# Recurrent segment attention beside a gated MLP: one projection moved to another group, small steps made list items, and new instruction lists

## Chip, cores, metric

One core of a Trainium2 chip. The metric is device time in microseconds for the whole program, the median of the runs. All weights and activations are bf16, sums are f32.

## The reference

x is 2048 tokens of 640 features. Two branches work on it and a gate mixes them.

```python
# A: 64 segments of 32 tokens, 32 heads of 192; 8 memory rows go from segment to segment
mem = mem0
for s in range(64):
    h = concat([mem, x[32 * s:32 * s + 32]])       # 40 rows
    q, k, v = h @ Wq, h @ Wk, h @ Wv               # 640 -> 32 heads x 192
    p = softmax(where(mask, q @ k.T / sqrt(192), -1e9))
    o = (p @ v) @ Wo                               # back to 640
    mem = o[:8]; out_s = o[8:]
# B: gated MLP, 640 -> 1536 -> 640
b = (gelu(x @ w_gate) * (x @ w_up)) @ w_down
g = sigmoid((x * gate_w).sum(-1))
return g * a + (1 - g) * b
```

Only the memory rows tie a segment to the one before, so the 64 segments are a serial chain. The mask lets the memory rows see everything and a token see the memory and the tokens up to itself.

## The kernel before

**Scheduler.** The source writes every operation with `S_.add(engine, ..., reads, writes)`, in one order for all engines. Each engine runs its own operations in that order; waits are derived from the regions read and written. Two engines that use one PSUM bank are always ordered, readers too. SP issues nearly all DMAs, in order as well, so an issue that waits holds those behind it. Every operation thus has a place in five queues: TensorE, ScalarE (ACT), VectorE (DVE), GpSimd (POOL) and SP.

**Stages.** First branch B runs in four blocks of 512 tokens (`ffn_transposes`, `ffn_gu`, `ffn_down`); its result goes to DRAM (`b_scr`), with the transposed x (`x_scr`, `xl_scr`) and the gate. Then come 64 calls of `segment(s)`.

**A segment.** A projection step works with 32 rows: the 8 memory rows that the segment before has just made, and the first 24 tokens. The last 8 tokens of each segment (the "left" rows) need no recurrence on the query side; they are projected for four segments at once, 32 rows at a time, and stored in DRAM (`qkl`). The 32 heads are four octets of 8 heads. `octet(s, i)` runs them forward in even segments and backward in odd ones, so i is the order in the segment. One projection of an octet, Q, K or V, has five pieces (k = 0 to 4) of 128 x 1536 weights; a piece is a quad: four matmuls of 384 columns, one for each 32-column strip of TensorE (L1121 where the stationary rows are loaded, L226 where they are kept from the matmul before).

**Lists.** `PROGS` holds four lists of items, one for each place of a segment in its group of four (place 1 is s % 4 == 0, place 4 is s % 4 == 3). An item is:

- `("g", n, k)`: piece k of every projection (m, i) in `GROUPS[n]`, with m = 0, 1, 2 for Q, K, V. They share one stationary: the first loads it, the others keep it. After the last k, ACT copies Q and K rows (L1141) and V (L1144) out of PSUM. In place 1 each V quad is followed by one for the left rows of V (`Vl`), copied by DVE (L1088).
- `("tq", i)`, `("tk", i)`: DVE transposes the rows of Q or K (L1155).
- `("sc", i)`: mask and scores (L1163, L1171, L1176), then on DVE maximum (L1189) and subtraction.
- `("ex", i)`: exponential on ACT, sum, reciprocal and product (L1207) on DVE.
- `("pt", i)`: TensorE transposes the probabilities; ACT copies them to PT.
- `("pv", i)`: P times V (L1254, L1256), into one PSUM bank (octet 3: two, A and B). ACT copies it to uT (L1265); in octet 3 DVE copies the middle third (L1270, "uT mid"). POOL then copies the left rows' part of uT into `uTl` (L1273).
- `("wo", i, h)`: output products of half an octet (L1283). Those of octet 3 go to a bank of their own (L1306). In place 4 every `wo` also multiplies `uTl` of four segments (`Wol`).
- `("lf", q, u, k)`: piece k of a left unit, that is Q and K of one octet for the left rows of the next group (L936, L226): two quads. `("le", q, u, m)`: ACT copies (L941) and DVE transposes (L943) it, SP stores it.
- `("vb", k)`: left rows of V for the next segment, in place 4.

**End of a segment.** The products of octets 0 to 2 lie in two halves of a bank: ACT copies one (`Zp`, L1289), DVE adds the other in two steps (`Zs`, L1292, `half_sums`), right behind item `("wo", 2, 1)`. After the list DVE adds octet 3's (`Za`, L1468) and transposes the memory rows (`Tm0`, L1472), on which the next segment's first quad waits; then the mix with b (`bz`) and the gate. What stands at the head of the next list as `lf`, or at the end of place 4 as `Wol`, is work that TensorE has meanwhile.

**Weights.** All weights but 16 pieces fit in SBUF at once. 13 pieces of Q, K and V of octet 0 share their space with the same pieces of octet 3, and three of Wo with three others; they are swapped in every segment by SP (L645) when TensorE has used them (`swap_loads`). Of one Q piece, `HALF`, only HX bytes per partition are swapped (L642). `out_store` and `x_load` are issued after the group with K of i = 1, `bz_load` and `bzl_load` (four DMAs) after the last `g` item.

## Time and profile before

| | us |
|---|---|
| Median of 3 runs | 1715.14 (1714.35 to 1719.47) |
| The profiled execution, its own time | 1719.43 |
| Its span, first to last instruction | 1717.6 |

| Engine | busy us | share |
|---|---|---|
| TensorE matmuls | 1589.8 | 93% |
| TensorE weight loads | 824.3 | 48% |
| VectorE | 955.7 | 56% |
| ScalarE | 800.4 | 47% |
| GpSimd | 340.2 | 20% |

The program moves 484.99 MB by DMA, 282 GB/s over the span. TensorE's granted clock is 0.997 on average. To read a profile row: the line of the kernel, engine and operation, then written and read tiles with their shapes; in groups a count, busy time and the mean in ns, and the idle time ahead of them with what ended it; in a timeline the start, the duration, and in square brackets the idle time ahead. [...]

### The profile page before, as it was taken

The page shows a single profiled execution, that of the slowest core. Times are in us where ns is not written, and L with a number is a line of the kernel's source. Part 1 is how long each engine was busy: PE and PEld are TensorE (multiplying, and loading weights), DVE is VectorE, ACT ScalarE, POOL GpSimd, SP SyncE. Part 2 cuts the span into 40 slices and gives each one's busy share as a digit, 9 for nine tenths or more (in the row PEclk, how much of TensorE's full clock was granted, in tenths as well). Part 3 has the DMA queues.
Part 4 walks back from the last instruction along what each step waited for, and adds up shares of the span by engine and source line. Part 5 has one row for each costly group of instructions (what it writes and reads, how often), then busy time and mean ns, then how long its engine had stood idle before and what let it go on. Part 6 is the DMA issues. An engine that isn't in the chain of part 4 may idle for free. (4 is left out here: it accounts for less than half of the span.)

```text
span 1717.6 us, 80494 instructions
## 1 busy us (share of the span) xinstructions
PE 1589.8 (93%) x39181; PEld 824.3 (48%) x31501; DVE 955.7 (56%) x2930; ACT 800.4 (47%) x1899; POOL 340.2 (20%) x1101
## 2 busy tenths in 40 slices
...
GB/s 326 316 53 137 290 303 310 291 265 288 299 303 292 274 300 292 322 280 277 275 305 311 276 309 269 302 301 280 288 286 299 296 305 265 297 292 310 275 278 258
DMA packets 273822, 484.99 MB, mean 282 GB/s; under 512 B 107686, under 2 KB 142782, under 8 KB 273470
## 3 DMA queue, kind: packets, MB, share of 16 engines
...
q14 instruction: 76, 0.62, 0.1%
...
## 5 line engine op out<-in xcount | busy, mean ns | idle before, releaser
L1121 PE MATMUL ps<-arena 128*32 128x384 bf16 x9940 | 710.0, 328 | 23.5 <-DVE arena L1472 12.3
L226 PE MATMUL ps<-arena 128*32 128x384 bf16 x7680 | 593.1, 327 | 12.7 <-ACT arena L1039 3.9
L1121 PEld LDWEIGHTS ps<-arena 128*32 128x32 bf16 x9940 | 253.8, 96 | 392.2 <-issue 259.6
L1155 DVE STREAM_TRANSPOSE arena<-arena 128x384 bf16<-128x384 bf16 x512 | 275.1, 561 | 149.4 <-ACT arena L1141 148.0
L1141 ACT ACTIVATE arena<-ps 128x384 bf16<-128x384 f32 x512 | 237.1, 490 | 223.9 <-PE ps L1121 210.0
L1283 PE MATMUL ps<-arena 128*32 128x320 bf16 x6144 | 278.5, 301 | 15.3 <-issue 12.7
L1265 ACT ACTIVATE arena<-ps 128x480 bf16<-128x480 f32 (+1 forms) x256 | 137.3, 536 | 174.8 <-PE ps L1256 163.8
L1283 PEld LDWEIGHTS ps<-arena 128*32 128x32 bf16 x6144 | 168.9, 107 | 72.6 <-issue 23.6
L1273 POOL COPY arena<-arena 128x96 bf16<-128x96 bf16 x256 | 89.9, 351 | 555.5 <-ACT arena L1265 506.7
L1144 ACT ACTIVATE arena<-ps 128x384 bf16<-128x384 f32 x256 | 125.1, 489 | 103.9 <-PE ps L1121 101.2
L1006 POOL COPY arena<-arena 128x96 bf16<-128x96 bf16 x256 | 68.4, 267 | 503.4 <-PE ps L1176 394.6
L1189 DVE TENSOR_REDUCE arena<-ps 104x4 f32<-104x160 f32 x256 | 82.7, 323 | 141.4 <-PE ps L1176 125.4
L1203 DVE TENSOR_REDUCE arena<-ps 104x4 f32<-104x160 f32 x256 | 80.6, 315 | 104.8 <-ACT ps L1201 102.5
L1239 ACT ACTIVATE arena<-ps 128x448 bf16<-128x448 f32 x192 | 104.0, 542 | 67.1 <-PE ps L1226 66.0
L1254 PE MATMUL ps<-arena 128*64 128x160 bf16 x1536 | 118.5, 243 | 6.8 <-ACT arena L941 3.3
L1201 ACT ACTIVATE ps<-ps 104x160 f32<-104x160 f32 x256 | 74.8, 292 | 102.6 <-DVE ps L1191 102.6
L1254 PEld LDWEIGHTS ps<-arena 128*64 128x64 bf16 x1536 | 79.6, 109 | 86.0 <-issue 28.7
L936 PE MATMUL ps<-arena 128*32 128x384 bf16 x1280 | 108.8, 328 | 0.1
L1256 PE MATMUL ps<-arena 128*64 128x64 bf16 x1536 | 102.0, 193 | 0.6 <-issue 0.6
L943 DVE STREAM_TRANSPOSE arena<-arena 128x384 bf16<-128x384 bf16 x128 | 73.0, 571 | 43.1 <-ACT arena L941 42.8
L1171 PE MATMUL ps<-arena 128*40 128x40 bf16 x2048 | 69.0, 182 | 26.3 <-DVE arena L1155 23.6
L1306 PE MATMUL ps<-arena 128*32 128x160 bf16 x3072 | 71.6, 233 | 23.0 <-DVE arena L1270 16.6
...
## 6 DMA issues: line engine op xcount, KB each, us to landing
...
arena<-in_A_Wq_dram SPq DMA_DIRECT2D x63, 144.0 KB, 3.3
...
```

Source lines behind the costliest of these rows:

```text
L226: return e.add_instruction(mybir.InstMatmult(name=nm, start_tensor_calc=like["start"], stop_tensor_calc=stop, tile_size=(128, 32), tile_po ...
L936: fns.append(lambda e, outp=outp, rhs=rhs, j=j: e.matmul(outp, lhs, rhs, start=(k == 0), stop=(k == KT - 1), tile_position=(0, 32 * j)))
L1121: fns.append(lambda e, outp=outp, rhs=rhs, j=j: e.matmul(outp, lhs, rhs, start=(k == 0), stop=(k == KT - 1), tile_position=(0, 32 * j)))
L1141: S_.add("act", lambda e, m=m, bk=bk: e.activation(out=rows_sb[m], in_=ps[:, bk, 0:384], func=ACTF.Copy), reads=[r_ps[bk]], writes=[r_rows ...
L1144: S_.add("act", lambda e, i=i, bk=bk: e.activation(out=v_sb[i % NVB].rearrange("p (c n) -> p c n", c=3), in_=ps[:, bk, 0:384].rearrange("p ...
L1155: S_.add("dve", lambda e: e.transpose(out=dst[:, :, 0:L], in_=rows_sb[m].rearrange("p (c r) -> p c r", r=L)), reads=[r_rows[m]], writes=[r ...
L1239: S_.add("act", lambda e: e.activation(out=PT, in_=ps[:, bank, 0:PTW + 128], func=ACTF.Copy), reads=[r_ps[bank]], writes=[r_PT], name="pT ...
L1254: return [lambda e: e.matmul(full, v[:, e0:e0 + 64], PTm[:, i], start=True, stop=False, tile_position=(0, 64 * i), skip_group_check=True), ...
L1256: lambda e: e.matmul(part, vl[:, e0:e0 + 64], PTl[:, i], start=False, stop=True, tile_position=(0, 64 * i), skip_group_check=True)]
L1265: S_.add("act", lambda e: e.activation(out=apx(u[:, 0, 0, :], [[R, na], [3 * R, 4], [1, R]]), in_=ps[:, A, 0:na * W].rearrange("p (c t r) ...
L1273: S_.add("pool", lambda e: e.tensor_copy(out=uTl[:, q, :, 12 * oc:12 * oc + 12].rearrange("p i (t c) -> p i t c", c=3), in_=u[:, :, :, L:R ...
L1283: fns.append(lambda e, i=i, t=t, j=j, gv=gv: e.matmul(ps[32 * j:32 * j + 32, bank, 0:2 * DJ].rearrange("p (h n) -> p h n", h=2), lhs2[i], ...
```

## The change

1. **Groups.** K of i = 2 joins the group of V of i = 1 and Q of i = 2: six groups instead of seven, and one load of the stationary per k less.
2. **uTl.** uT keeps the 32 token rows alone. The left rows go straight from PSUM to `uTl` by DVE, in place of POOL's copy from uT. The copy reads the bank that ACT reads for uT, and so comes after it.
3. **Items.** `zp` and `zs` (the two half sums), `ou` (`out_store`), `xt` (`x_load`) and `bz` (`bz_load`) are items with places of their own. `outl_store` follows `("sc", 2)` in place 1.
4. **Left rows of b.** `bl_copy` lays them out in DRAM (`bl_scr`) so that `bzl_load` is one DMA, now in place 4 after group 1.
5. **Left units.** Place 1 has none; its unit, octet 3, goes to place 3, which has two.
6. **Memory.** Freed space makes HX 384 instead of 1152 bytes.
7. **Prologue.** In block 0 the transposed x is copied out of PSUM after each 128 tokens, in turn from two sets of banks. The gate's DVE transposes (`gate_turn`) come after the third left unit instead of the first.
8. **New lists** for all four places.

The core of the diff; of the old lists their last lines only:

```diff
-    GROUPS = [[(0, 0), (1, 0)], [(2, 0), (0, 1), (1, 1)], [(2, 1), (0, 2)], [(1, 2)], [(2, 2), (0, 3)], [(1, 3)], [(2, 3)]]
...
-         ("g", 5, 2), ("g", 5, 3), ("wo", 0, 0), ("g", 5, 4), ("tq", 3), ("pt", 1), ("g", 6, 0), ("tk", 3),
-         ("lf", 0, 1, 0), ("lf", 0, 1, 1), ("ex", 2), ("pv", 1), ("sc", 3), ("wo", 0, 1), ("pt", 2), ("g", 6, 1),
-         ("lf", 0, 1, 2), ("ex", 3), ("pv", 2), ("lf", 0, 1, 3), ("g", 6, 2), ("g", 6, 3), ("g", 6, 4), ("pt", 3),
-         ("lf", 0, 1, 4), ("le", 0, 1, 0), ("wo", 1, 0), ("wo", 1, 1), ("pv", 3), ("wo", 2, 0), ("le", 0, 1, 1),
-         ("wo", 2, 1), ("wo", 3, 0), ("wo", 3, 1)],
...
-         ("wo", 0, 0), ("ex", 2), ("g", 5, 4), ("pv", 1), ("tk", 3), ("sc", 3), ("g", 6, 0), ("lf", 1, 1, 3),
-         ("pt", 2), ("wo", 0, 1), ("g", 6, 1), ("g", 6, 2), ("ex", 3), ("lf", 1, 1, 4), ("pv", 2), ("g", 6, 3),
-         ("pt", 3), ("g", 6, 4), ("wo", 1, 0), ("le", 1, 1, 0), ("wo", 1, 1), ("pv", 3), ("le", 1, 1, 1),
-         ("wo", 2, 0), ("wo", 2, 1), ("wo", 3, 0), ("wo", 3, 1)],
...
-         ("lf", 2, 1, 4), ("g", 5, 2), ("g", 5, 3), ("tq", 3), ("g", 5, 4), ("tk", 3), ("g", 6, 0), ("pt", 2),
-         ("g", 6, 1), ("sc", 3), ("le", 2, 1, 0), ("ex", 3), ("wo", 1, 0), ("g", 6, 2), ("pv", 2), ("wo", 1, 1),
-         ("wo", 2, 0), ("pt", 3), ("g", 6, 3), ("g", 6, 4), ("wo", 2, 1), ("pv", 3), ("le", 2, 1, 1), ("wo", 3, 0),
-         ("wo", 3, 1)],
...
-         ("tq", 3), ("g", 5, 1), ("g", 5, 2), ("g", 5, 3), ("g", 5, 4), ("wo", 0, 0), ("pt", 2), ("tk", 3),
-         ("g", 6, 0), ("sc", 3), ("g", 6, 1), ("wo", 0, 1), ("g", 6, 2), ("pv", 2), ("wo", 1, 0), ("ex", 3),
-         ("g", 6, 3), ("wo", 1, 1), ("g", 6, 4), ("vb", 0), ("vb", 1), ("pt", 3), ("wo", 2, 0), ("pv", 3),
-         ("wo", 2, 1), ("wo", 3, 0), ("wo", 3, 1), ("vb", 2), ("vb", 3), ("vb", 4)]]
+    GROUPS = [[(0, 0), (1, 0)], [(2, 0), (0, 1), (1, 1)], [(2, 1), (0, 2), (1, 2)], [(2, 2), (0, 3)], [(1, 3)], [(2, 3)]]
+        [("g", 0, 0), ("g", 0, 1), ("g", 0, 2), ("g", 0, 3), ("ou", 0), ("g", 0, 4), ("g", 1, 0), ("g", 1, 1),
+         ("tq", 0), ("g", 1, 2), ("tk", 0), ("sc", 0), ("g", 1, 3), ("ex", 0), ("g", 1, 4), ("g", 2, 0), ("g", 2, 1),
+         ("g", 2, 2), ("tq", 1), ("pt", 0), ("g", 2, 3), ("tk", 1), ("g", 2, 4), ("sc", 1), ("pv", 0), ("g", 3, 0),
+         ("g", 3, 1), ("g", 3, 2), ("g", 3, 3), ("tq", 2), ("tk", 2), ("ex", 1), ("sc", 2), ("g", 3, 4),
+         ("wo", 0, 0), ("pt", 1), ("g", 4, 0), ("ex", 2), ("g", 4, 1), ("g", 4, 2), ("g", 4, 3), ("g", 4, 4),
+         ("tq", 3), ("g", 5, 0), ("g", 5, 1), ("xt", 0), ("tk", 3), ("pv", 1), ("wo", 0, 1), ("pt", 2), ("sc", 3),
+         ("ex", 3), ("pv", 2), ("g", 5, 2), ("g", 5, 3), ("g", 5, 4), ("pt", 3), ("wo", 1, 0), ("wo", 1, 1),
+         ("bz", 0), ("pv", 3), ("wo", 2, 0), ("wo", 2, 1), ("zp", 0), ("wo", 3, 0), ("zs", 0), ("wo", 3, 1)],
+        [("lf", 1, 0, 0), ("lf", 1, 0, 1), ("lf", 1, 0, 2), ("g", 0, 0), ("g", 0, 1), ("g", 0, 2), ("g", 0, 3),
+         ("g", 0, 4), ("tq", 0), ("lf", 1, 0, 3), ("g", 1, 0), ("tk", 0), ("lf", 1, 0, 4), ("g", 1, 1),
+         ("le", 1, 0, 0), ("sc", 0), ("g", 1, 2), ("g", 1, 3), ("le", 1, 0, 1), ("ex", 0), ("ou", 0), ("g", 1, 4),
+         ("g", 2, 0), ("g", 2, 1), ("tq", 1), ("tk", 1), ("g", 2, 2), ("pt", 0), ("g", 2, 3), ("sc", 1), ("pv", 0),
+         ("ex", 1), ("g", 2, 4), ("wo", 0, 0), ("wo", 0, 1), ("xt", 0), ("g", 3, 0), ("g", 3, 1), ("pt", 1),
+         ("bz", 0), ("g", 3, 2), ("g", 3, 3), ("tk", 2), ("tq", 2), ("g", 3, 4), ("g", 4, 0), ("g", 4, 1), ("sc", 2),
+         ("g", 4, 2), ("tq", 3), ("g", 4, 3), ("g", 4, 4), ("tk", 3), ("g", 5, 0), ("lf", 1, 1, 0), ("ex", 2),
+         ("lf", 1, 1, 1), ("lf", 1, 1, 2), ("g", 5, 1), ("sc", 3), ("pv", 1), ("g", 5, 2), ("pt", 2),
+         ("lf", 1, 1, 3), ("ex", 3), ("lf", 1, 1, 4), ("le", 1, 1, 0), ("pv", 2), ("pt", 3), ("g", 5, 3),
+         ("g", 5, 4), ("le", 1, 1, 1), ("wo", 1, 0), ("wo", 1, 1), ("pv", 3), ("wo", 2, 0), ("wo", 2, 1), ("zp", 0),
+         ("wo", 3, 0), ("zs", 0), ("wo", 3, 1)],
+        [("lf", 2, 0, 0), ("xt", 0), ("lf", 2, 0, 1), ("g", 0, 0), ("lf", 2, 0, 2), ("g", 0, 1), ("lf", 2, 0, 3),
+         ("lf", 2, 0, 4), ("le", 2, 0, 0), ("g", 0, 2), ("g", 0, 3), ("g", 0, 4), ("tk", 0), ("tq", 0),
+         ("le", 2, 0, 1), ("g", 1, 0), ("g", 1, 1), ("g", 1, 2), ("g", 1, 3), ("g", 1, 4), ("sc", 0), ("g", 2, 0),
+         ("g", 2, 1), ("tq", 1), ("tk", 1), ("g", 2, 2), ("ex", 0), ("ou", 0), ("g", 2, 3), ("g", 2, 4), ("sc", 1),
+         ("tk", 2), ("g", 3, 0), ("pt", 0), ("g", 3, 1), ("g", 3, 2), ("tq", 2), ("ex", 1), ("g", 3, 3), ("pv", 0),
+         ("g", 3, 4), ("sc", 2), ("g", 4, 0), ("g", 4, 1), ("lf", 2, 1, 0), ("pt", 1), ("tq", 3), ("ex", 2),
+         ("g", 4, 2), ("lf", 2, 1, 1), ("g", 4, 3), ("wo", 0, 0), ("g", 4, 4), ("lf", 2, 1, 2), ("tk", 3),
+         ("lf", 2, 1, 3), ("lf", 2, 1, 4), ("pv", 1), ("sc", 3), ("wo", 0, 1), ("g", 5, 0), ("le", 2, 1, 0),
+         ("bz", 0), ("pt", 2), ("g", 5, 1), ("g", 5, 2), ("g", 5, 3), ("ex", 3), ("pv", 2), ("wo", 1, 0),
+         ("g", 5, 4), ("wo", 1, 1), ("pt", 3), ("wo", 2, 0), ("wo", 2, 1), ("zp", 0), ("pv", 3), ("zs", 0),
+         ("wo", 3, 0), ("le", 2, 1, 1), ("wo", 3, 1)],
+        [("g", 0, 0), ("g", 0, 1), ("g", 0, 2), ("g", 0, 3), ("g", 0, 4), ("g", 1, 0), ("g", 1, 1), ("tk", 0),
+         ("tq", 0), ("g", 1, 2), ("g", 1, 3), ("g", 1, 4), ("ou", 0), ("sc", 0), ("g", 2, 0), ("tq", 1), ("g", 2, 1),
+         ("tk", 1), ("g", 2, 2), ("ex", 0), ("g", 2, 3), ("g", 2, 4), ("sc", 1), ("pt", 0), ("tq", 2), ("g", 3, 0),
+         ("g", 3, 1), ("g", 3, 2), ("tk", 2), ("g", 3, 3), ("ex", 1), ("pv", 0), ("sc", 2), ("g", 3, 4), ("pt", 1),
+         ("g", 4, 0), ("ex", 2), ("g", 4, 1), ("g", 4, 2), ("wo", 0, 0), ("g", 4, 3), ("tq", 3), ("wo", 0, 1),
+         ("g", 4, 4), ("g", 5, 0), ("pv", 1), ("pt", 2), ("g", 5, 1), ("tk", 3), ("pv", 2), ("g", 5, 2), ("sc", 3),
+         ("g", 5, 3), ("wo", 1, 0), ("wo", 1, 1), ("xt", 0), ("ex", 3), ("bz", 0), ("pt", 3), ("g", 5, 4), ("vb", 0),
+         ("wo", 2, 0), ("pv", 3), ("vb", 1), ("wo", 2, 1), ("zp", 0), ("zs", 0), ("wo", 3, 0), ("wo", 3, 1),
+         ("vb", 2), ("vb", 3), ("vb", 4)]]
-    HX = 1152
+    HX = 384
-    LUNIT = ({1: 3}, {0: 1, 1: 0}, {1: 2}, {})
+    LUNIT = ({}, {0: 1, 1: 0}, {0: 2, 1: 3}, {})
...
-        S_.add("act", lambda e: e.activation(
-            out=apx(u[:, 0, 0, :], [[R, na], [3 * R, 4], [1, R]]),
-            in_=ps[:, A, 0:na * W].rearrange("p (c t r) -> p c t r", t=4, r=R), func=ACTF.Copy),
-            reads=[r_ps[A]], writes=[ru[0]] if na == 2 else ru, name="uT evac s%d o%d" % (s, o))
+        S_.add("act", lambda e: e.activation(out=u.rearrange("p t c r -> p c t r")[:, 0:na], in_=pa[:, 0:na, :, 0:L], func=ACTF.Copy),
+               reads=[r_ps[A]], writes=[ru[0]] if na == 2 else ru, name="uT evac s%d o%d" % (s, o))
...
+            S_.add("dve", lambda e: e.tensor_copy(out=ul[:, :, :, 2], in_=pb[:, 2, :, L:R].rearrange("p t i -> p i t")),
+                   reads=[r_ps[B]], writes=[r_uTl[q][oc]], name="uTl mid s%d o%d" % (s, o))
-        S_.add("pool", lambda e: e.tensor_copy(
-            out=uTl[:, q, :, 12 * oc:12 * oc + 12].rearrange("p i (t c) -> p i t c", c=3), in_=u[:, :, :, L:R].rearrange("p t c i -> p i t c")),
-            reads=[r_uT[o % NUB]], writes=[r_uTl[q][oc]], name="uTl s%d o%d" % (s, o))
+        S_.add("dve", lambda e: e.tensor_copy(out=ul[:, :, :, 0:na], in_=pa[:, 0:na, :, L:R].rearrange("p c t i -> p i t c")),
+               reads=[r_ps[A]], writes=[r_uTl[q][oc]], name="uTl s%d o%d" % (s, o))
...
+    def bl_copy(blk):
+        v = b_scr[blk * FB:(blk + 1) * FB].rearrange("(s t) n -> s t n", t=L)
+        for j in range(4):
+            S_.add("sp", lambda e, j=j: e.dma_start(
+                bl_scr[4 * blk:4 * blk + 4, j].rearrange("g (q i) n -> g q i n", i=M),
+                v[:, XA:L, DJ * j:DJ * (j + 1)].rearrange("(g q) i n -> g q i n", q=4)),
...
```

133 lines of the change are left out of this document (80 added, 53 removed), and 23 rows, old and new, of the table PROGS.

## The prediction

> **What bounds the kernel now.** I read the page's head, then the stretches of the loop, then who TensorE waits for, then the timeline at those waits.
>
> ```profile
> span 1717.6 us, 80494 instructions
> 209.20:1688.80 1479.60, 1368.06 (x36740) 713.44 (x29360) 877.19 (x2751) 726.85 (x1760) 312.58 (x1022) 1.00 0.83 291
> 855.20:878.89 23.69, 23.36 (x635) 11.96 (x500) 16.09 (x50) 12.11 (x30) 4.20 (x16) 1.00 0.81 286
> 878.89:902.69 23.80, 21.86 (x586) 10.61 (x450) 14.61 (x46) 12.42 (x30) 4.87 (x17) 1.00 0.86 300
> 902.69:926.27 23.58, 20.68 (x544) 10.08 (x428) 13.54 (x44) 11.69 (x28) 5.46 (x17) 1.00 0.83 299
> 926.27:950.28 24.01, 22.81 (x628) 13.71 (x530) 12.55 (x42) 10.78 (x27) 5.54 (x18) 1.00 0.81 288
> ...
> PE ps L1171 <- DVE arena L1155: 23.6, 45, 0.8
> PE ps L1306 <- DVE arena L1270: 16.6, 16, 1.2
> PE ps L1306 <- DMA arena<-in_A_Wo_dram: 4.3, 9, 1.5
> ```
>
> The columns of a stretch are its length, then busy time and count for TensorE, its weight loads, VectorE, ScalarE and GpSimd, then granted clock, DMA share, GB/s. The second line is 62 segments (23.86 us each); the four below are segments 28 to 31, places one to four, from one segment's first projection to the next's. TensorE is busy 87 to 99% of them at clock 1.00. Its matmul counts differ because the left units are spread unevenly: 635, 586, 544, 628. So the kernel is bound by one in-order TensorE list, and its time is that work plus the moments in which the list's next item isn't ready. VectorE, busy 14.2 us of 23.8 on average (56.78 over the four), makes nearly all of those moments: transposed rows come late for scores (23.6 us), the middle third of uT comes late for the last output products (16.6 us, 16 times: once in every third place). Transfers cost little directly (4.3 us in the largest named row).
>
> The price of work, for what follows:
>
> ```profile
> 909.14 0.34 PE L226 MATMUL ps<-arena 128*32 128x384 bf16 x4
> 909.30 0.50 PE L1121 MATMUL ps<-arena 128*32 128x384 bf16 x8
> ...
> 910.32 0.25 PE L1163 MATMUL ps<-arena 128*40 128x160 bf16 x2
> 910.46 0.28 PE L1171 MATMUL ps<-arena 128*40 128x40 bf16 x8
> 910.87 0.67 PE L1121 MATMUL ps<-arena 128*32 128x384 bf16 x12
> ...
> 912.61 0.26 PE L1254 MATMUL ps<-arena 128*64 128x160 bf16 x2
> 912.66 0.29 DVE L1207 TENSOR_TENSOR arena<-ps,arena 104x128 bf16<-104x128 f32 x1
> 913.03 0.35 PE L936 MATMUL ps<-arena 128*32 128x384 bf16 x4
> ...
> L1270 DVE CAST arena<-ps 128x160 bf16<-128x160 f32 x64 | 20.3, 317 | 24.2 <-PE ps L1256 24.1
> L1235 DVE CAST arena<-ps 128x128 bf16<-128x128 f32 x64 | 18.5, 288 | 27.0 <-PE ps L1226 27.0
> L1265 ACT ACTIVATE arena<-ps 128x480 bf16<-128x480 f32 x192 | 109.4, 570 | 132.5 <-PE ps L1256 123.1 <-POOL arena L1008 6.3 <-PE ps L1121 1.8
> ```
>
> A quad (four matmuls of 384 columns side by side) costs 0.16 us: 909.14 to 909.30. A scores item costs 0.55 (910.32 to 910.87), a PV item 0.42 (912.61 to 913.03). From scores to finished probabilities takes about 2.5 us (910.46 to 912.66 plus the 0.29 of that row).
>
> **The change, part by part.**
>
> *K of octet 2 on the stationary of V1 and Q2.* The loads saved (20 per segment, in five quads) are worth nothing. In the fence, a quad that keeps its stationary (L226) is followed after 0.16 us, and two quads that load one each (L1121, x8) take 0.50, that is 0.16 more than one. Loads already run under matmuls. [...] Moving K2 forward does help its chain, but octet 2's scores are not among the large waits now.
>
> *uTl from PSUM by VectorE, not from uT by GpSimd.* VectorE gains three copies of 96 columns, and in octet 3 one of 64 and one of 32. Its two rows above give 0.9 ns a column, hence about 260, 230 and 200 ns (estimates), 1.2 us a segment. uT shrinks from 480 to 384 columns on ScalarE, about 0.08 us off the 570 ns row. VectorE has room, but its queue is in order: each uTl waits for ScalarE's uT copy of the same bank, and what is queued behind (transposes, softmax sums) waits too. The kernel's scheduler orders any two engines on one bank. [...] It speaks against the change, and gives the first rival.
>
> *Place 3's end and its new units.*
>
> ```profile
> 923.37 0.20 PE L1256 MATMUL ps<-arena 128*64 128x64 bf16 x2
> 923.58 0.67 DVE L1292 TENSOR_TENSOR arena<-ps,arena 64x160 f32<-64x160 f32 x2 [1.06 <-PE ps L1256]
> 924.17 0.31 DVE L1270 CAST arena<-ps 128x160 bf16<-128x160 f32 x1
> 924.63 1.01 PE L1306 MATMUL ps<-arena 128*32 128x160 bf16 x48 [1.06 <-DVE arena L1270]
> 925.69 0.25 DVE L1468 TENSOR_TENSOR arena<-ps,arena 128x64 bf16<-128x64 f32 x1 [0.24 <-PE ps L1306]
> 926.27 0.35 PE L1121 MATMUL ps<-arena 128*32 128x384 bf16 x4 [0.63 <-DVE arena L1472]
> ...
> 904.99 0.33 PE L226 MATMUL ps<-arena 128*32 128x384 bf16 x4 [0.17 <-ACT arena L1141]
> 918.68 0.28 PE L1171 MATMUL ps<-arena 128*40 128x40 bf16 x8 [0.46 <-DVE arena L1155]
> 921.47 0.26 PEld L1283 LDWEIGHTS ps<-arena 128*32 128x32 bf16 x12 [0.48 <-ACT arena L1265]
> ```
>
> Today the two half sums (L1292) stand ahead of the uT middle on VectorE: 1.06 us idle. Boundary: 0.63 idle. Scores 3: 0.46, plus 0.17 in which the last quad only drains (a quad shows 0.34 but costs 0.16). Smaller: 0.17 and about 0.4. Together about 2.9. In the new list the sums follow PV3, but the ScalarE half "zp" still stands ahead of its uT copy, and uTl, the sums and then the left transpose ("le" before the last "wo") come before Z. I walk it from PV3's end with the rows' durations: Wo of octet 3 starts about 0.5 late, Z leaves the boundary 1.2 idle, and PV2 comes 0.25 after its pT copy would let it. About 2.0. Scores 3 has six left quads and a PV ahead (1.4 us) and no longer waits. The ten extra quads (1.6 us) that come from place 1 fill holes such as the two small ones. Place 3, its own work set apart: −1.3 us (from −0.8, by the large rows alone, to −1.5).
>
> *Place 2.*
>
> ```profile
> 892.74 0.34 PE L1121 MATMUL ps<-arena 128*32 128x384 bf16 x4
> 893.13 0.49 ACT L1141 ACTIVATE arena<-ps 128x384 bf16<-128x384 f32 x1 [0.66 <-PE ps L1121]
> 893.65 0.58 DVE L1155 STREAM_TRANSPOSE arena<-arena 128x384 bf16<-128x384 bf16 x1 [0.18 <-ACT arena L1141]
> 894.29 0.28 PE L1171 MATMUL ps<-arena 128*40 128x40 bf16 x8 [0.72 <-DVE arena L1155]
> ...
> 877.62 0.38 PE L936 MATMUL ps<-arena 128*32 128x384 bf16 x4
> 878.89 0.35 PE L1121 MATMUL ps<-arena 128*32 128x384 bf16 x4
> ...
> 901.41 0.34 PE L936 MATMUL ps<-arena 128*32 128x384 bf16 x4
> 902.69 0.35 PE L1121 MATMUL ps<-arena 128*32 128x384 bf16 x4
> ```
>
> From the last K quad to scores 3 the chain copy, transpose takes 1.55 us (892.74 to 894.29), and only PV1 stands between: 0.72 idle. The new list has eight quads there (1.3): that wait goes. At the boundary two quads (0.33) fill 1.28 us (901.41 to 902.69): 0.95 lost. New: no left transposes ahead of Z and four quads, 0.4 lost. What is late next: pT3. After scores 3 stand a PV, a V quad, a pT, four left quads and a PV (2.0 us); but the exponential is queued on ScalarE behind the uT copy of octet 1 and the PT copy of octet 2, which pushes the 2.5 us to above 3. About 0.75 late, and PV2 0.15. Place 2: −0.72 −0.55 +0.9 = −0.4; with waits of 0.1 to 0.2 between its items that the better cover takes, −0.6.
>
> *Place 1.* Boundary now: four quads (0.65) in 877.62 to 878.89, 0.62 lost; new six quads and no left transposes ahead of Z, 0.2 lost: −0.4. But its left unit was filler. In the new list K3, scores 3 and pT3 follow each other with only V and PV between; octet 2's softmax, both transposes and uTl queue on VectorE. I walk it to scores 3 0.45 late and pT3 0.45 late. Place 1: +0.5 beside its 1.6 us less work, which place 3 has back.
>
> *Place 4.* PV2 comes one quad after pT2, and the PT copy that it needs is no shorter than the 0.49 of the row at 893.13, with a uT copy ahead of it on ScalarE: +0.8. Scores 3, late today, get about 0.5 more cover. +0.3.
>
> *Transfers and queues.* The swapped part of one Q piece shrinks from 1152 to 384 bytes a partition.
>
> ```profile
> arena<-in_A_Wq_dram SPq DMA_DIRECT2D x63, 144.0 KB, 3.3
> ...
> 178.29 0.33 PE L226 MATMUL ps<-arena 128*32 128x384 bf16 x4 [0.95 <-ACT arena L941]
> ```
>
> 96 KB less each segment at 291 GB/s is 0.34 us of queue, 21 us over 63 if transfers set the pace, nothing if not. TensorE's waits on transfers are some us in all: 2 us. Out store and x load move to items behind the V swaps on SP's queue; bzl becomes one load in place of four; cover is the slack before x copy. 0. The DRAM copy of left rows ("bl copy") is 16 issues in 1700 us, behind stores long landed: 0. Gate transposes leave VectorE's queue ahead of the left transposes in the prologue: that frees the 0.95 us at 178.29, once. The split xT copies save under 1 us, which the first weights' arrival hides: 0.
>
> **Sum.** Per four segments +0.5 −0.6 −1.3 +0.3 = −1.1; 15.75 times −17 us; with the prologue −18; I leave the 2 us of transfers as margin. The profiled execution took 1719.4 us (span and 1.8 around it), the top of the three runs (1714.35 to 1719.47); the sum gives 1701 for it. Against the median of 1715.14, the same step gives 1697.
>
> **Rivals.**
>
> *VectorE's queue decides (slower).* Every uTl holds the queue from PV's end until ScalarE's copy is done (570 ns now) and then 260 ns. I charged this at the ends and at octets 2 and 3. If in each segment two further places, say the octet 1 and 2 transposes, come 0.35 late, that is 45 us: 1742. From 0.28 us a segment on it eats the gain. For: 23.6 us of waits hang on L1155 already. Against: scores 0 to 2 have long cover, and VectorE is idle 40%. 0.17.
>
> *Transfers take over.* A shorter segment with the same swaps leaves less time to land (DMA share 0.81 to 0.86 already); half of the gain turns into waits on Wo and V: 1707. 0.16.
>
> *The walk is too dark in places 1 and 4.* The late pT3 and PV2 there don't come, so 0.5 and 0.8 go: −38 us, 1677. 0.13.
>
> *The lists don't fit the banks.* Three products at once in group 2 need a third free bank beside left ones, and TensorE waits for evacuations as at 904.99 (0.17 to 0.34) wherever it happens; the merge then gives nothing back and gains cancel: 1715. 0.06.
>
> *Loads count after all.*
>
> ```profile
> L1121 PEld LDWEIGHTS ps<-arena 128*32 128x32 bf16 x9940 | 253.8, 96 | 392.2 <-issue 259.6 <-DVE arena L1472 60.2 <-ACT arena L1141 4.9
> ```
>
> Five quads of loads fewer a segment, 96 ns each with its four side by side, none hidden: 64 x 5 x 0.096 = 31 us more gain, 1666. 0.02, since the 0.16 us between quads contradicts it. [...]
>
> **How the numbers follow.** Forecast 0.46. Faster by over 0.3% (5.1 us, about what can be told from no change): most of the forecast (0.41), 0.13, 0.02, and two thirds of the transfers' case, 0.10: 0.66. Same: 0.03 of the forecast, 0.05, 0.05: 0.13. Slower: 0.02, 0.01, 0.01, 0.17: 0.21. The range drops half of the slower rival and the far end of the fast ones: 1678 to 1728. The forecast's own: 1688 to 1708, from place 3 at −0.8 to −1.5 and place 1 and 4 by 0.2 each way.
>
> **What the changed profile would show.** Right: the row of Wo's last octet waiting for the uT middle (16.6 us) falls under 8; scores waiting for L1155 (23.6) falls by half or more, its rest in place 1; waits of pT for probabilities grow above 15 us; VectorE up by 70 us (1.2 x 64 less the shorter uT middle), GpSimd down; place 3 lasts under 24 us with about 640 matmuls. Wrong: sum of PE's waits unchanged, or waits on Wo and V pieces above 20 us, or scores 1 and 2 waiting for transposes.

## The result, and the profile after

The changed kernel takes 1708.35 us (median of seven runs, 1703.70 to 1712.39) where the kernel before takes 1718.08 on the same chip (1714.35 to 1727.34): the ratio of the means is 0.9935, 95% interval 0.9908 to 0.9963. Run again for the experiments, it took 1704.29 (1700.25 to 1708.93), 0.991 (0.9892 to 0.9928). By these ratios it is 11 to 15 us faster; the forecast step was 18. The forecast's 1697 started from a median of 1715.14 for the kernel before; from the 1718.08 measured here the same step gives 1700. The profiled execution took 1703.7 us.

The head of its profile and the stretches of the loop (62 segments, then segments 28 to 31, places one to four; columns as before):

```profile
span 1701.8 us, 79166 instructions
PE 1568.4 (92%) x39180; PEld 791.4 (47%) x30220; DVE 996.0 (59%) x3256; ACT 783.6 (46%) x1902; POOL 251.3 (15%) x845
...
207.72:1672.30 1464.58, 1348.10 (x36768) 681.82 (x28129) 916.42 (x3062) 710.72 (x1762) 226.46 (x774) 1.00 0.82 290
851.41:875.17 23.76, 22.30 (x606) 11.50 (x468) 15.61 (x53) 11.42 (x28) 3.42 (x12) 1.00 0.79 282
875.17:898.06 22.89, 21.46 (x590) 9.82 (x428) 15.33 (x51) 12.20 (x30) 3.00 (x12) 1.00 0.85 303
898.06:921.20 23.14, 21.22 (x577) 9.99 (x426) 15.10 (x51) 12.06 (x30) 3.84 (x13) 1.00 0.86 302
921.20:945.88 24.68, 22.73 (x628) 13.00 (x512) 13.49 (x48) 10.64 (x27) 4.29 (x14) 1.00 0.77 276
```

The loop is 1464.58 us against 1479.60: 15 us, so nearly the whole gain lies there. Four segments are too few to read a place by, since one place differs from group to group by over 1 us. The means over all segments between the second and the last, taken from the starts of first projections in each trace, in us:

| kernel | place 1 | 2 | 3 | 4 | sum |
|---|---|---|---|---|---|
| before | 24.33 | 23.54 | 23.09 | 24.55 | 95.51 |
| after | 23.71 | 23.08 | 23.32 | 24.43 | 94.54 |
| after, run again | 23.48 | 23.41 | 23.18 | 24.47 | 94.54 |

The sum repeats within 0.01, one place within about 0.3. Counted from first projection to first projection, eight quads went from place 1 to place 3 in every group but the last (7.5 on average, 1.2 us at 0.1625 each; two of the unit's ten are only a matter of where a place begins). With that set apart, the two profiles give place 1 +0.6 and +0.4, place 2 −0.5 and −0.1, place 3 −1.0 and −1.1, place 4 −0.1 and −0.1.

Who TensorE waits for now:

```profile
PE ps L1145 <- DVE arena L1505: 22.9, 37, 1.2
PE ps L1245 <- DVE arena L1231: 15.5, 33, 0.7
PE ps L1278 <- ACT arena L1263: 14.3, 39, 0.7
PE ps L1195 <- DVE arena L1179: 11.7, 17, 1.5
PE ps L1145 <- DMA arena<-in_A_Wv_dram: 10.3, 26, 0.6
PE ps L1333 <- ACT arena L1063: 8.3, 16, 0.5
```

The two rows that led before are half as long: scores for transposed rows 23.6 to 11.7 (L1195), Wo of octet 3 16.6 to 8.3 (L1333; the row names ScalarE's gate copy, but the timeline shows the uT copy just ahead of it ending last). Longer are first projections waiting for the state (L1505, 12.3 before), pT for probabilities (L1231, 8.6), PV for its PT copy (L1263, 0.9) and quads for V pieces (1.6).

TensorE's idle time in the loop did not fall: 111.5 us before (1479.60 less 1368.06), 116.5 now; its busy time fell by 20 us for the same matmuls. A quad that ends in a wait shows 0.34 us and one followed at once costs 0.16, so a wait behind a quad hides 0.18 us of itself in the busy column. The clearest case is the mask, which stands ahead of the scores that it belongs to. Over the 62 segments (248 octets) the time from the start of the mask to the start of the scores adds up to 59.1 us before, and to 36.5 and 34.1 in the two profiles after; it is 0.08 us where nothing waits, 20 us in all. So 23 to 25 us were won there, of which the idle column shows 14 to 17 (27.0 before, 13.4 and 9.9 after). Places 2 and 4 won it (22.9 to 6.0 and 13.9 to 4.8 us in the first profile), place 3 did not (16.2 to 18.4, and 15.0 in the second).

The scores that still wait are thus in another place than forecast: ahead of scores 3 in place 3 TensorE idles 11.0 us (7.6 in the second profile), and from start to start 13 us (10) are lost there. The timeline of one (segment 14), VectorE, TensorE and SyncE's queue:

```profile
523.68 0.78 SPq L970 DMA_DIRECT2D left_qk_scratch<-arena  x1
...
532.41 0.26 DVE L1299 CAST arena<-ps 128x96 bf16<-128x96 f32 x1 [3.10 <-PE ps L956]
532.58 0.32 DVE L1213 TENSOR_REDUCE arena<-ps 104x4 f32<-104x160 f32 x1
532.93 0.33 DVE L1215 TENSOR_TENSOR ps<-ps,arena 104x160 f32<-104x160 f32 x1
533.17 0.57 DVE L1179 STREAM_TRANSPOSE arena<-arena 128x384 bf16<-128x384 bf16 x1
...
534.50 0.57 DVE L1179 STREAM_TRANSPOSE arena<-arena 128x384 bf16<-128x384 bf16 x1
535.12 0.28 PE L1195 MATMUL ps<-arena 128*40 128x40 bf16 x8 [1.50 <-DVE arena L1179]
```

The uTl copy of octet 0 (L1299, VectorE) starts at 532.41. ScalarE's copy of the same bank had ended at 529.26, so the engine named in brackets isn't the releaser. What ended then was a transfer: the left unit's store, issued at 523.68, landed at 532.29. The rows of a left unit are kept in the part of uTl's memory that place 3 writes, and the first uTl copy of place 3 may not overwrite them before the store has read them. Behind it on VectorE stand the softmax of octet 2 and both transposes of octet 3, and so scores 3. VectorE's own waits name it seven times, up to 2.7 us:

```profile
L1299 DVE CAST arena<-ps 128x96 bf16<-128x96 f32 (+1 forms) x256 | 63.5, 248 | 96.0 <-ACT arena L1292 43.5 <-DMA left_qk_scratch<-arena 12.8 <-PE ps L1145 9.1
...
left_qk_scratch<-arena SPq DMA_DIRECT2D x49, 192.0 KB, 7.5
```

The left unit that moved to place 3 brought this: nothing in the prediction priced its store.

### The profile page after: what moved, and what is told of

It is laid out like the page before. It is cut to its first block, busy times and chain, and to the rows that moved or that the text cites. A ratio compares the mean times of both kernels' runs of the same rounds, so it can differ in the third digit from the quotient of the medians.

```text
span 1701.8 us, 79166 instructions
## 1 busy us (share of the span) xinstructions
PE 1568.4 (92%) x39180; PEld 791.4 (47%) x30220; DVE 996.0 (59%) x3256; ACT 783.6 (46%) x1902; POOL 251.3 (15%) x845
## 4 chain that ended last, share of the span: by engine, by line
PE 62%; DMA 21%; DVE 9%; ACT 4%; issue 3%; SPq 0%; DVEq 0%; ACTq 0%
PE ps L226 15%; PE ps L1145 14%; DMA arena<-in_A_Wv_dram 12%; PE ps L1308 10%; DMA left_qk_scratch<-arena 5%; DMA arena<-in_A_Wo_dram 3%; PE ps L872 3%; PE ps L869 3%; PE ps L1278 3%; PE ps L887 2%; PE ps L1333 2%; DVE arena L1319 2%; PE ps L1200 2%; PE ps L956 2%; PE ps L1187 1%
## 5 line engine op out<-in xcount | busy, mean ns | idle before, releaser
L1145 PE MATMUL ps<-arena 128*32 128x384 bf16 x8660 | 653.5, 328 | 42.1 <-DVE arena L1505 22.9
L226 PE MATMUL ps<-arena 128*32 128x384 bf16 x8960 | 633.0, 326 | 5.3 <-DVE arena L1319 3.5
L1145 PEld LDWEIGHTS ps<-arena 128*32 128x32 bf16 x8660 | 226.0, 96 | 404.5 <-issue 261.2
L1179 DVE STREAM_TRANSPOSE arena<-arena 128x384 bf16<-128x384 bf16 x512 | 269.0, 557 | 102.5 <-ACT arena L1165 100.0
L1165 ACT ACTIVATE arena<-ps 128x384 bf16<-128x384 f32 x512 | 229.7, 490 | 195.7 <-PE ps L1145 186.2
L1308 PE MATMUL ps<-arena 128*32 128x320 bf16 x6144 | 271.4, 301 | 8.6 <-issue 7.4
L1308 PEld LDWEIGHTS ps<-arena 128*32 128x32 bf16 x6144 | 170.6, 107 | 64.1 <-issue 15.2
L1168 ACT ACTIVATE arena<-ps 128x384 bf16<-128x384 f32 x256 | 125.3, 489 | 139.9 <-PE ps L1145 132.5
L1292 ACT ACTIVATE arena<-ps 128x384 bf16<-128x384 f32 (+1 forms) x256 | 118.8, 464 | 150.3 <-PE ps L1280 139.3
L1031 POOL COPY arena<-arena 128x96 bf16<-128x96 bf16 x256 | 69.4, 271 | 643.8 <-PE ps L1200 425.8
L1278 PE MATMUL ps<-arena 128*64 128x160 bf16 x1536 | 118.8, 242 | 16.9 <-ACT arena L1263 14.3
L1263 ACT ACTIVATE arena<-ps 128x448 bf16<-128x448 f32 x192 | 104.7, 545 | 64.2 <-PE ps L1250 61.6
L1299 DVE CAST arena<-ps 128x96 bf16<-128x96 f32 (+1 forms) x256 | 63.5, 248 | 96.0 <-ACT arena L1292 43.5
L1227 DVE TENSOR_REDUCE arena<-ps 104x4 f32<-104x160 f32 x256 | 78.5, 306 | 51.4 <-ACT ps L1225 51.2
L956 PE MATMUL ps<-arena 128*32 128x384 bf16 x1280 | 107.4, 328 | 0.0
L805 POOL COPY arena<-arena 128x120 bf16<-128x120 bf16 x64 | 18.4, 287 | 558.8 <-PE ps L1308 137.8
L963 DVE STREAM_TRANSPOSE arena<-arena 128x384 bf16<-128x384 bf16 x128 | 72.7, 568 | 37.4 <-ACT arena L961 36.7
L961 ACT ACTIVATE arena<-ps 128x384 bf16<-128x384 f32 x128 | 62.4, 491 | 64.6 <-PE ps L956 53.2
```

The costliest lines, as they stand in the source:

```text
L226: return e.add_instruction(mybir.InstMatmult(name=nm, start_tensor_calc=like["start"], stop_tensor_calc=stop, tile_size=(128, 32), tile_po ...
L956: fns.append(lambda e, outp=outp, rhs=rhs, j=j: e.matmul(outp, lhs, rhs, start=(k == 0), stop=(k == KT - 1), tile_position=(0, 32 * j)))
L1145: fns.append(lambda e, outp=outp, rhs=rhs, j=j: e.matmul(outp, lhs, rhs, start=(k == 0), stop=(k == KT - 1), tile_position=(0, 32 * j)))
L1165: S_.add("act", lambda e, m=m, bk=bk: e.activation(out=rows_sb[m], in_=ps[:, bk, 0:384], func=ACTF.Copy), reads=[r_ps[bk]], writes=[r_rows ...
L1168: S_.add("act", lambda e, i=i, bk=bk: e.activation(out=v_sb[i % NVB].rearrange("p (c n) -> p c n", c=3), in_=ps[:, bk, 0:384].rearrange("p ...
L1179: S_.add("dve", lambda e: e.transpose(out=dst[:, :, 0:L], in_=rows_sb[m].rearrange("p (c r) -> p c r", r=L)), reads=[r_rows[m]], writes=[r ...
```

## The experiments

Each ran beside the kernel before, which took 1717.57 to 1719.38 us in the four groups. Times are medians, ratios are to the kernel before, places are means as above. The places come from the one profiled execution, whose own time stands beside the median; it is 6 to 8 us below the median in split_store, own_rows and late_v, and 6 to 7 us above it in store_act and swap_1152, so read their places with that in mind. The first four rows are one group, then four, three and one; "after run again" is in the first alone, so a difference to it from another group carries the 2 us by which the kernel before differs between them.

| run | us | profiled | ratio, 95% interval | places 1 to 4 |
|---|---|---|---|---|
| after, run again | 1704.29 | 1703.48 | 0.9910, 0.9892 to 0.9928 | 23.48, 23.41, 23.18, 24.47 |
| k2_loads | 1710.95 | 1708.73 | 0.9945, 0.9929 to 0.9960 | 24.10, 23.33, 23.20, 24.26 |
| sums_ahead | 1708.00 | 1706.27 | 0.9935, 0.9910 to 0.9959 | 23.67, 23.07, 23.64, 24.47 |
| split_store | 1713.34 | 1707.10 | 0.9965, 0.9942 to 0.9987 | 23.51, 23.19, 23.89, 24.18 |
| store_act | 1749.51 | 1755.08 | 1.0173, 1.0141 to 1.0205 | 23.55, 23.46, 26.38, 24.35 |
| swap_1152 | 1704.38 | 1711.76 | 0.9909, 0.9882 to 0.9936 | 23.79, 23.47, 23.26, 24.47 |
| skip_piece | 1695.17 | 1695.13 | 0.9875, 0.9853 to 0.9896 | 23.74, 22.95, 22.81, 24.36 |
| utl_gpsimd | 1729.06 | 1728.84 | 1.0075, 1.0050 to 1.0100 | 23.74, 23.43, 23.21, 25.91 |
| own_rows | 1700.56 | 1692.46 | 0.9893, 0.9863 to 0.9923 | 23.58, 23.21, 22.98, 24.19 |
| late_v | 1729.08 | 1721.13 | 1.0063, 1.0038 to 1.0088 | 23.52, 23.01, 23.66, 25.65 |
| combo2 | 1723.46 | 1721.65 | 1.0046, 1.0024 to 1.0068 | 23.61, 23.19, 23.15, 25.90 |
| own_rows_vl | 1744.21 | 1738.57 | 1.0152, 1.0112 to 1.0191 | 23.74, 23.03, 23.14, 27.12 |

**The baseline.** 

> The changed kernel once more, as the baseline of the three beside it. Both theories: 1708 us within 4, third places 23.3 us on average, from first projection to first projection.

As expected.

**Loads of the merged stationary.**

```diff
-                   ... mms(m, bk, htile(k), k, g_, n > 0),
+                   ... mms(m, bk, htile(k), k, g_, n > 0 and (m, i) != (1, 2)),
```

> The order of all work stays; only K of octet 2 loads its stationary anew (20 weight loads more in each segment, 1280 in all), although the one it needs stands there. Theory A (loads run under matmuls of 384 columns): 0, within 4 us of the changed kernel beside it, quads still 0.16 us apart. Theory B (loads count): 96 ns for the four loads of a quad, 5 quads in 64 segments, 31 us slower; a quarter of that would be 8 us.

```profile
L1145 PEld LDWEIGHTS ps<-arena 128*32 128x32 bf16 x9940 | 261.0, 96 | 395.2 <-issue 224.1
```

The row has 1280 loads more than after (8660). Over the 315 quads of K of octet 2 after the first segment, the quad starts 0.162 us after the one ahead of it and what follows starts 0.163 us after it (medians), loaded here and kept in after: the loads lie under the matmuls. Yet the run is 6.7 us slower than after run again, with intervals that just miss each other. TensorE's waits on nothing that the profile shows ("issue") add up to 28.6 us here and to 20.5 and 23.2 in the two profiles of after, which is of that size; but skip_piece, which has the kept loads, shows 28.8 as well. Whether 1280 instructions more cause it stays open. It is not 31 us.

**Half sums ahead of PV3 in place 3.**

```diff
-         ("wo", 2, 1), ("zp", 0), ("pv", 3), ("zs", 0),
+         ("wo", 2, 1), ("zp", 0), ("zs", 0), ("pv", 3),
```

> In place 3 both half sums go back ahead of the last PV item, where they stood in the kernel before; nothing else changes. Theory A (as the prediction had it): the uT middle waits behind the sums again, Wo of octet 3 starts 0.5 us later in each third place, 8 us in the program. Theory B (the left transpose sets the end): the left transpose before Z is free 0.6 us after the first output product anyway; with the sums done early the end of the place is bound by Wo alone, the boundary gives back about 0.4, and the net is 0.1 to 0.2 us a third place, 2 us in all.

```profile
PE ps L1333 <- DVE arena L1297: 16.8, 15, 1.2
```

Each theory has a part of it. Wo of octet 3 waits 16.8 us, as in the kernel before (16.6), 8.5 more than after. But the sums are then out of VectorE's way, and the time from the last output product to the next first projection falls from 1.14 and 1.09 us to 0.87, some 4 us over 16 places. Net, place 3 is 0.3 to 0.5 longer and the median 4 us higher, with intervals that overlap: the order of the sums is likely worth half of what the wait row says.

**The store in two halves.** The K half goes to the memory of place 4, the Q half is stored earlier.

```diff
+    lx_off = [o_ul + 2 * UTQ, o_ul + 3 * UTQ]
...
-        half = s % 4 == 2 and u == 1
+        half = s % 4 == 2
```

> The left unit that moved from place 1 into the head of place 3 (left group of octet 2, or its counterpart) is written to two halves with a DMA store each, the Q half in the uTl area of place 3 (stored some 2.5 us earlier, ahead of five or six weight swaps) and the K half in the area of place 4, which nobody writes for 20 us. Nothing else changes. Theory A (store): VectorE's first uTl copy of each third place waits until the left unit's store has read its rows out of the same memory (12 to 14 us after the segment's start in the profile), VectorE's queue is in order, and so the sums and transposes of octets 2 and 3 come late; scores 3 of place 3 waits 13 us in all for that. Then the wait of VectorE for the left store (12.8 us, 7 times in the profile after) goes, scores 3 no longer waits, third places shorten by 0.5 to 0.9 us, the program by 8 to 14 us. Theory B (late weight pieces): K pieces of octet 3 land late and hold scores 3 back; they come as before, so third places change by less than 0.2 us, the program by less than 3 us.

Neither theory held. The uTl copy now starts 0.08 us after ScalarE's copy (1.83 in after, means), and scores 3 waits in one place only (0.9 us), but place 3 is longer and the run some 9 us slower than after run again.

```profile
PE ps L1150 <- DMA arena<-in_A_Wv_dram: 21.3, 44, 1.3
```

Another wait took its place: V pieces of octet 3 (21.3 us; 10.3 and 13.7 in the profiles of after). The swapped pieces land one after the other, about 1 us apart, from 4 us after the start of place 3 to near its end. The fourth of the five V pieces lands 16.2 us into the place in before, 16.9 in after, 17.9 here. The store in place 3 stands ahead of them on SyncE's queue, which likely makes up the first 0.7 us. In two halves it costs another 1.0: the Q half now waits for its transpose ahead of six swaps (the first of these is issued 3.3 instead of 2.1 us into the place), and there are 7920 more packets in the program, of rows half as long. The two were not told apart.

**The store on ScalarE's queue.**

```diff
-            left_store(*unit(s, u), 3)
+            left_store(*unit(s, u), 3, "act" if s % 4 == 2 else AUXQ)
```

> The left unit's store at the head of place 3 is issued by ScalarE's queue instead of SyncE's, where it stands behind eight weight swaps; one store of the same shape, nothing else changed. ScalarE has nothing to do at that moment (from its last row copy to the exponential of octet 0, some 2 us). Theory A (store, then transfers): the store lands some 5 us earlier, VectorE's wait for the left store (5 to 13 us in the profiles) goes to 0, scores 3 of place 3 no longer waits; but the V pieces of octet 3 come no earlier, and half of it turns into waits on them: program 3 to 8 us faster than the changed kernel, third places 23.0. Theory B (the split store was slower for its own bytes alone, and transfers have slack without them): all 13 us of scores 3 are won, third places 22.5, 12 us faster. Theory C (transfers set the pace of place 3 wholly): V waits take all of it, within 3 us.

All three were wrong about the landing, and it is the clearest run for the mechanism:

```profile
DVE arena L1299 <- DMA left_qk_scratch<-arena: 58.1, 14, 4.9
...
left_qk_scratch<-arena SPq DMA_DIRECT2D x34, 192.0 KB, 7.6
left_qk_scratch<-arena ACTq DMA_DIRECT2D x15, 192.0 KB, 10.4
```

On a queue of its own the store lands later, 10.4 us after its issue. VectorE's wait grows from 12.8 to 58.1 us, place 3 by 3.1 us, the program by 45, and no other place moves. In this place the landing of a store sets the pace.

The longer wait is not the whole price. TensorE idles 45.1 us ahead of scores 3 in place 3, 34 to 37 more than in the two profiles of after. Behind most of these waits its granted clock falls to half, as in segment 14 (in the windows, columns as before; the clock is the third from the end):

```profile
544.08 0.28 PE L1195 MATMUL ps<-arena 128*40 128x40 bf16 x8 [3.03 <-DVE arena L1179]
...
544.48 0.59 PE L1308 MATMUL ps<-arena 128*32 128x320 bf16 x12
544.90 0.34 PE L1145 MATMUL ps<-arena 128*32 128x384 bf16 x4
...
546.68 0.99 PE L1308 MATMUL ps<-arena 128*32 128x320 bf16 x12
547.46 0.54 PE L1145 MATMUL ps<-arena 128*32 128x384 bf16 x4
...
541.00:545.60 4.60, 1.57 (x54) 1.09 (x52) 3.67 (x13) 1.66 (x5) 0.00 (x0) 1.00 0.76 301
545.60:549.02 3.42, 3.35 (x62) 1.97 (x58) 1.31 (x7) 1.61 (x5) 0.29 (x1) 0.50 0.76 179
```

Twelve output products take 0.42 us to the next start at 544.48 and 0.78 at 546.68. In the loop 51.2 us run at half clock, 44.4 of them in place 3, against 6.8 and 17.1 in the profiles of after. If half of the extra 34 to 44 us is lost work, that is 17 to 22 us (an estimate); with the longer waits it makes 51 to 59 us, and the loop of the profiled execution is 51 us longer.

The packets of the two traces show how the store comes to land late. In after its 512 packets of 384 bytes start between 4.5 and 7.2 us after the issue, with 265 swap packets of 3072 bytes among them (means of 15 places). From ScalarE's queue they start 3.9 us after the issue, a little sooner, but go on until 9.8 us after it, with 685 swap packets among them. So the store begins 0.6 us earlier and its last packet starts 2.6 us later, with 2.6 times as many large packets of the swaps between its own.

**A larger swap.**

```diff
-    HX = 384
+    HX = 1152
```

> The swapped part of the Q piece is 1152 bytes a partition again, as in the kernel before: 96 KB more in each segment, 0.2 to 0.34 us of transfer. Nothing else changes. Theory A (transfers set the pace in the second half of most segments): V pieces of octet 3 land that much later, TensorE's waits on them (10 to 14 us) and VectorE's wait for the left store grow; 8 to 16 us slower than the changed kernel. Theory B (as the prediction had it): the 2 us of margin, within 4 us.

Theory B: 1704.38 in the median of four, the same as without it. That part of the change buys nothing that can be measured.

**One swap less.**

```diff
+            if other[0] == 1 and other[2] == 0:
+                loaded[slot_id[other]] = other
+                continue
             load_piece(other, "swap s%d" % seg)
```

> Leaves out one of the sixteen weight swaps of each segment (the K piece with k = 0; the octets that need it use stale weights), 384 KB or 0.93 us of transfer a segment less. All else stays. Theory A (transfers are late): every later piece and the left store land up to 0.9 us earlier; TensorE's waits on weight pieces (17 to 20 us in all) and VectorE's wait for the left store go; 15 to 30 us faster than the changed kernel. Theory B (transfers hidden but for the named waits on V): 5 to 10 us.

9 us faster than after run again, as theory B had it (this kernel leaves one weight piece out and computes with an old one, so only its time counts): in place 3 the V pieces land 0.3 to 0.6 us earlier than in the two profiles of after, the store at 12.30 instead of 13.04 and 12.78 us into the segment, waits on V fall to 7.0 us, and place 3 gains most (22.81). Transfers are late by an amount that one swap of sixteen changes, but not everything waits for them.

**uTl by GpSimd again.**

```diff
-        S_.add("dve", lambda e: e.tensor_copy(out=ul[:, :, :, 0:na], in_=pa[...L:R]...
+        S_.add("pool", lambda e: e.tensor_copy(out=ul, in_=u[:, :, :, L:R]...
```

> GpSimd copies uTl out of a uT of 40 columns again, as in the kernel before; the lists stay. The larger uT takes 384 bytes a partition, so the swapped part of Q is 768 bytes, 48 KB or 0.12 us of transfer more in each segment. Theory A (VectorE pays for uTl only through the store): VectorE does 60 us less, GpSimd waits for the left store in its place, scores 3 of place 3 no longer waits, which wins 8 to 13 us, and the larger swap costs 2 to 5: 4 to 10 us faster than the changed kernel. [...]

Theory A failed by 30 us.

```profile
PE ps L1145 <- DMA arena<-in_A_Wv_dram: 22.6, 49, 1.0
...
PE ps L1306 <- POOL arena L1297: 14.5, 14, 1.7
```

Scores 3 of place 3 hardly waits any more (0.8 us), but quads wait for V pieces instead (8.1 us in place 3, 0.7 and 1.7 in after), and place 3 is as long as before the edit. Place 4 is 1.45 us longer: its left output products (L1306) come right behind Wo of octet 3 in the new list and wait for GpSimd's uTl of the same octet. That row is 14.5 of the some 22 us; the rest was not taken apart. With the new lists the copy on VectorE is worth 25 us; without it the change would have been slower than before.

**Rows of their own.**

```diff
-    wsB["uTl"] = 4 * UTQ
+    wsB["uTl"] = 5 * UTQ
...
-    HX = 384
+    HX = 1152
...
-    lst_off = [... wsB_off["v"], o_ul + 2 * UTQ]
+    lst_off = [... wsB_off["v"], o_ul + 3 * UTQ]
```

> The left unit at the head of place 3 (and those of place 2) keep their transposed rows in memory of their own instead of the uTl area of place 3; the 768 bytes a partition for it come from a swapped Q part of 1152 instead of 384 bytes. The store stays one store at the same place of SyncE's queue, nothing else changes. VectorE's first uTl copy of a third place then has no DMA to wait for. Theory A (one wait takes the place of the other): scores 3 of place 3 no longer waits (11 to 13 us in the changed kernel), but the V pieces of octet 3 land at the same time and now hold TensorE 8 to 12 us in place 3; third places within 0.2 us of 23.2, the program within 4 us of the changed kernel. Theory B (the store's wait is a loss by itself): third places 22.5, 10 us faster.

The rows are 1536 bytes a partition and move by 768: one half lies in the new memory, the other in place 4's part of uTl, which nothing writes during place 3. Closer to A: 3.7 us faster than after run again, in another group of runs. The store's wait is gone (the uTl copy starts 0.10 us after ScalarE's). In place 3 TensorE idles 1.0 us ahead of scores 3 (11.0 and 7.6 in after) and 5.2 us for V pieces (0.7 and 1.7), and the place is 0.2 to 0.3 shorter. It is the fastest of the whole kernels here, 0.9893 of before; against the changed kernel the intervals overlap (0.9892 to 0.9928), so that step is likely, not shown.

**A new second half of place 3, V later, the left transpose behind Z.**

```diff
- ("wo", 0, 1), ("g", 5, 0), ... ("pv", 2), ("wo", 1, 0), ("g", 5, 4), ("wo", 1, 1), ("pt", 3),
- ("wo", 2, 0), ("wo", 2, 1), ("zp", 0), ("pv", 3), ("zs", 0), ("wo", 3, 0), ("le", 2, 1, 1), ("wo", 3, 1)
+ ("wo", 0, 1), ("wo", 1, 0), ("g", 5, 0), ... ("wo", 1, 1), ... ("pv", 2), ("pt", 3), ("g", 5, 4),
+ ("wo", 2, 0), ("pv", 3), ("wo", 2, 1), ("zp", 0), ("zs", 0), ("wo", 3, 0), ("wo", 3, 1), ("le", 2, 1, 1)
```

> Only the second half of place 3's list changes: both output products of octet 1 come ahead of the V quads of octet 3 (V is needed 0.4 to 0.8 us later), PV3 goes one output product earlier so that Wo of octet 3 has an output product to cover ScalarE's uT copy, and the left transpose comes after the last output product and so behind Z on VectorE. Theory A (order): waits on V pieces in place 3 go, Wo of octet 3 waits 0.2 instead of 0.6 us, the boundary gives back 0.3 to 0.4; third places 0.7 to 1.0 us shorter, 11 to 16 us. The wait for the left store stays. Theory B (VectorE or ScalarE late again: the probabilities of octet 3 or the sums before Z): under 0.3 us a place, under 5 us.

25 us slower, by neither theory. Place 3 got longer, as the half sums now end after the last product (from its start to the next first projection it is 1.28 us, 1.14 and 1.09 in after), and place 4 lost 1.2 us. SyncE's queue at the start of place 4 tells why, in after and here (segment 31; first projections at 921.20 and 924.14):

```profile
920.75 0.37 SPq L975 DMA_DIRECT2D left_qk_scratch<-arena  x1
921.17 0.50 SPq L1025 DMA_DIRECT2D arena<-left_qk_scratch  x1
921.74 0.42 SPq L646 DMA_DIRECT2D arena<-in_A_Wk_dram  x1
```

```profile
925.33 0.37 SPq L975 DMA_DIRECT2D left_qk_scratch<-arena  x1
925.75 0.51 SPq L1025 DMA_DIRECT2D arena<-left_qk_scratch  x1
926.30 1.82 SPq L646 DMA_DIRECT2D arena<-in_A_Wk_dram  x1
```

The store of the last left rows waits for that transpose; behind it on the in-order queue stand the stage load and every weight swap of place 4. The first swap is issued 2.2 instead of 0.5 us into the place, and K pieces hold TensorE 13.2 us (2.9 in after). So the left transpose is worth its place ahead of Z: 1.2 us behind the boundary.

**Both, with an output product ahead of PV2 in place 4.** The third edit:

```diff
- ("tk", 3), ("pv", 2), ("g", 5, 2), ("sc", 3), ("g", 5, 3), ("wo", 1, 0), ("wo", 1, 1)
+ ("tk", 3), ("wo", 1, 0), ("pv", 2), ("g", 5, 2), ("sc", 3), ("g", 5, 3), ("wo", 1, 1)
```

> Both edits beside it together (rows of their own, the new second half of place 3), and in place 4 the first output product of octet 1 between pT2 and PV2. Theory A (waits in series: with V later and no store in VectorE's way, nothing takes the place of the wait): third places 22.0 to 22.4, fourth places 0.3 to 0.5 shorter for the PV2 wait of 0.63; 20 to 27 us faster than the changed kernel. Theory B (weight transfers set the pace): the shorter places make later pieces late in places 4 and 1, and half of it is left, 8 to 14 us.

Place 4 lost as in late_v, for the same reason (K pieces 15.0 us). There the third edit only moved a wait: PV2 of place 4 no longer waits for its PT copy (9.1 us in late_v), but pT3, which the output product had covered, waits 14.6 us for the probabilities (1.1 in late_v). What it would do where the weights are on time isn't shown.

**Left V ahead of PV2 in place 4, on rows of their own.**

```diff
- ("g", 5, 1), ("tk", 3), ("pv", 2), ("g", 5, 2), ("sc", 3), ... ("vb", 0), ("wo", 2, 0), ("pv", 3), ("vb", 1)
+ ("g", 5, 1), ("vb", 0), ("tk", 3), ("vb", 1), ("g", 5, 2), ("pv", 2), ("sc", 3), ... ("wo", 2, 0), ("pv", 3)
```

> The kernel with rows of their own for the left units, and in place 4 the first two quads of the left V (which need pieces that are there already) and one V quad of octet 3 moved between pT2 and PV2, where TensorE waits 0.8 us in each fourth place for ScalarE's PT copy (12.8 us in all). Theory A (order): that wait falls under 4 us, fourth places go from 24.2 to 23.7, 6 to 9 us faster than the kernel with rows of their own. Theory B (transfers or the place's end take it back): the quads are missed ahead of Wo of octet 3, or pieces of places 4 and 1 come late; under 3 us.

```profile
PE ps L1118 <- DMA arena<-left_x_scratch: 40.4, 15, 3.5
```

The wait of PV2 fell as in theory A (its row from 11.9 to 2.2 us), and a larger one came: the left V quads also need the next group's left x, whose load stands behind the swaps and lands 17.4 us into place 4 (mean in own_rows). The expectation had looked at the weight pieces only. As in store_act, the clock falls to half behind most of these waits, here in segment 31:

```profile
950.77 0.51 PE L1118 MATMUL ps<-arena 128*32 128x384 bf16 x8 [2.62 <-DMA arena<-left_x_scratch]
...
951.80:955.21 3.41, 3.41 (x66) 2.21 (x62) 1.71 (x7) 0.77 (x2) 0.00 (x0) 0.50 0.24 82
```

In the loop 54.6 us run at half clock, 51.2 of them in place 4; in own_rows it is 13.7.

## Why the prediction was right in direction and 3 to 7 us too large

*Place 1, +0.5 forecast, +0.6 and +0.4 measured.* The sum fits, half of its terms don't. pT3 comes 0.4 late (forecast 0.45) and the boundary gives back 0.3 (0.4); scores 3, 0.45 in the walk, waits about 0.1, and PV2 (0.3), V pieces (0.1 to 0.2) came instead.

*Place 2, −0.6 forecast, −0.5 and −0.1.* Ahead of scores more went than the 0.72 forecast, 1.06 us from mask to scores; the boundary gave 0.3 (0.55). The late pT3 came as the walk had it: behind PV2 it starts 0.80 us after the item ahead of it (0.81 in the second profile) where 0.15 is usual, so 0.65 late (0.75 forecast), and the exponential does stand on ScalarE behind the uT copy of octet 1 and the PT copy of octet 2. In segment 29:

```profile
891.00 0.49 ACT L1292 ACTIVATE arena<-ps 128x384 bf16<-128x384 f32 x1 [2.07 <-PE ps L1280]
891.39 0.54 ACT L1263 ACTIVATE arena<-ps 128x448 bf16<-128x448 f32 x1
891.82 0.30 ACT L1225 ACTIVATE ps<-ps 104x160 f32<-104x160 f32 x1
...
893.07 0.22 PE L1245 MATMUL ps<-arena 104*32 104x80 bf16 x4 [0.60 <-DVE arena L1231]
```

The sum had no term for waits on V pieces of octet 3 (0.3 us a place) and of Wo for the uT copy (0.2).

*Place 3, −1.3 forecast, −1.0 and −1.1.* The sum does not give −1.3: its terms are 2.9 before and 2.0 after, −0.9, and the small holes that the extra quads were to fill are in the 2.9 already. Wo of octet 3 starts 0.52 late (forecast 0.5) and the boundary idles 0.90 and 0.86 (1.2). "Scores 3 … no longer waits" was the step that failed: 0.8 and 0.6 us a place are lost there, as in the kernel before (0.7), through the store that came along with the moved left unit and the uTl copy that now stands in VectorE's queue. The prediction counted the unit's ten quads as free filler, and not its DMA, although uTl's row and the store's row of before were there to read. With these sizes the sum gives −0.4 to −0.6. The rest of the gain comes from waits that it did not list: quads take 0.8 to 0.9 us more where 7.5 more of them cost 1.2, PV3 waits 0.2 less, and the output products of octets 0 to 2 take 0.5 to 0.6 less, of which it had about 0.4. That the number is near is in part luck. Taking the store's wait away alone wins little (own_rows), because V pieces take back half of it.

*Place 4, +0.3 forecast, −0.1.* PV2 waits 0.61 and 0.65 (0.8), and 0.6 went ahead of scores (0.5). What the sum had no term for is a wait that goes: in the kernel before pT of octet 1 idles 0.51 us a place here for the probabilities (7.7 of the 8.6 us of that row), now nothing. GpSimd's uTl would make this place 1.45 us longer in the new list (utl_gpsimd), so part 2 of the change is needed for it. The price of the copy was right: 63.5 us and 14.1 us (the middle's) of VectorE are the 1.2 us a segment. The rows of VectorE's groups add up to 66 us more than before, near the 70; the head, which counts overlapping instructions once, shows 40.

*Transfers, "2 us in all".* This term was mis-sized. Named waits on weight pieces rose from 7.2 to 17.4 us (20.1 in the second profile), nearly all of it on V, and a sixteenth of the swaps is worth 9 us (skip_piece). The rival "Transfers take over", 1707 us, describes this in part: a shorter segment with the same swaps gives some of what the order won back to waits on V pieces, though not on Wo. The results (1708.35 and 1704.29) are nearer to it than to 1697. Shrinking the Q swap bought nothing, as forecast.

*K2's loads, 0 forecast.* The spacing of quads bears it out: 0.162 and 0.163 us, whether the stationary is loaded (k2_loads) or kept (after). The 31 us of the rival did not come; 6.7 us, unexplained, did.

*The rival that VectorE's queue decides* was the right mechanism with the wrong trigger: not ScalarE's copy, for which VectorE does wait 43.5 us (without that copy on VectorE, in utl_gpsimd, places 1 and 2 are no shorter), but a store. At 1.9 us of mean delay in 15 of 64 segments it cost 13 us or less; at 4.2 us (store_act) the program takes 45 more, part of it at half clock, and is slower than before. VectorE is also not "nearly all" of the waits: before, its rows hold 64 of the loop's 103 us, and 22 us are waits on nothing that the profile shows.

*The checks named.* Kept: scores waiting for transposes by half, pT above 15 us, place 3 under 24 us, GpSimd down (340.2 to 251.3). Missed: that its rest lies in place 1; Wo of octet 3 under 8 (8.3); place 3 has 577 matmuls, not 640 (544 and ten quads would have been 584). "Sum of PE's waits unchanged" was named as a sign of being wrong; it happened (113.8 us before, 122.8 and 120.2 after), and the time still fell, because these rows leave out what a wait hides in the matmul ahead of it, above all in the mask ahead of scores. Time from start to start would have been the better sign.

*Open:* why the store's packets start only 4 us after its issue even from a queue of its own (3.9 us in store_act); the 6.7 us of k2_loads; the split xT copies and the gate transposes in the prologue were not tried alone (the first projection of the second segment came at 208.96 before, 207.72 and 208.44 after, and anywhere from 205.8 to 209.5 in the other runs, so the 1 us forecast for them can't be told).
